# Float64 weights to float32: a byte-to-integer operation on ACT in place of two operations on DVE

## The chip, the cores and the metric

One core of one Trainium2 chip runs the kernel. The metric is the device time in microseconds (us) of one execution; lower is better.

## What is computed

A local and a downsampled attention over 4 batches x 8 heads x 576 positions x 64, then a gated feed-forward layer, then a second one with a layer norm. Only the weights of the last two matter for the change. They reach the kernel as float64:

```python
k = np.maximum(xk @ w_k, 0.0)            # xk: 2304 x 512, w_k: 512 x 1024
v = k * k @ w_v                          # w_v: 1024 x 512
r = 1.0 / (1.0 + np.exp(-(xr @ w_r)))    # w_r: 512 x 512
x = r * v
...
ch = np.maximum(xn @ w_ch1, 0.0) @ w_ch2 # w_ch1: 512 x 2048, w_ch2: 2048 x 512
out = x + ch
```

## The kernel before

**Weights.** Every weight matrix is cut into tiles of 128 x 512: 4 of `w_r`, 8 of `w_k`, 8 of `w_v`, 16 each of `w_ch1` and `w_ch2`, together 52. `load_f32` brings one in as raw float64 (512 KB) into a buffer called `w64` (in the trace `w`, and the order listings number it), of which there are two. It then makes a float32 tile `wf` (two buffers) out of the high and the low 32-bit word of each number: an absolute value on ACT, then four DVE operations that clamp, shift and mask the high word, put the top three bits of the low word under it, and put the sign on top. `load_split` splits `wf` into a rounded part (name ending in `h`) and a remainder (`l`), since every matrix product is three products of float32r parts (lines L741 to L743). The first 20 tiles, `w_r`, `w_k` and `w_v`, are needed in the first 150 us; the 32 of `w_ch1` and `w_ch2` come between 275 and 446 us.

**The rest of the start.** The attention of the first batch (four units of two heads) must be through before the first product of the feed-forward layer: its results are added into `xT` (L725), mixed with the previous position into `tmu` (L765) and split into `xr`, `xk` (L769). Then come `psr` (with `w_r`), `psk` (with `w_k`) and `psv` (with `w_v`) in PSUM, between them the attention of later batches. Where PE would have nothing to do early on, small products called `warm` (L417) are put in.

**Order.** A planner (`Plan`) holds all operations with an engine, a cost and a due time, and lists them; operations that two engines can do (copies, remainders) go where the plan has them end sooner. Each engine runs its own list strictly in order. All DMAs are issued from one queue, SP, also in order: a load of a weight waits there until DVE is done with the buffer, and everything listed behind it waits too.

Of the kernel before, what the change touches and what calls it, by code (L numbers as in the profile page):

```python
# [3 lines left out]

# [6 lines left out]
F32 = mybir.dt.float32  # L11
F32R = mybir.dt.float32r
U32 = mybir.dt.uint32
BF16 = mybir.dt.bfloat16
AF = mybir.ActivationFunctionType
ALU = mybir.AluOpType
# [2 lines left out]

P = 128  # L20
NEG = -8.0e9

TINY = struct.unpack("<f", struct.pack("<I", 896 << 20))[0]


PRM = dict(
# [34 lines left out]
class Plan:  # L61
# [15 lines left out]
    def add(self, eng, cost, prio, fn, r=(), w=(), lat=0.0, port=False, thin=False):  # L77
        ways = [(eng, cost, fn, port)] if isinstance(eng, str) else eng
        op = Op(len(self.ops), ways, prio, lat, thin)
        for kind, items in (("r", r), ("w", w)):  # L80
            for it in items:
                b, key = it if isinstance(it, tuple) else (it, None)
                keys = set(b.writer) | set(b.readers) if key is None else {key, None}
                for kk in keys:
                    if kk in b.writer:
                        op.deps.add(b.writer[kk])
                    if kind == "w":
                        op.deps.update(b.readers.get(kk, ()))
                if b not in op.bufs:
                    op.bufs.append(b)  # L90
        for it in r:
            b, key = it if isinstance(it, tuple) else (it, None)
            b.readers.setdefault(key, []).append(op.i)
        for it in w:
            b, key = it if isinstance(it, tuple) else (it, None)
            if key is None:
                b.writer.clear()
                b.readers.clear()
            b.writer[key] = op.i
            b.readers[key] = []  # L100
        op.deps.discard(op.i)
        self.ops.append(op)
# [138 lines left out]
def c_act(n, psum=False, ap=0):  # L241
    return (0.05 if psum else 0.093) + n / 1200 + 0.093 * ap


def c_dve(n, fast=False):
    return 0.066 + n / (1920 if fast else 960)
# [6 lines left out]
def c_dma(nbytes, small=False):  # L253
    return max(0.41, nbytes / 360e3 * (2 if small else 1))
# [3 lines left out]
def attn_moe_kernel(  # L258
# [15 lines left out]
    nc = tc.nc  # L274
# [18 lines left out]
    add = plan.add  # L293
# [22 lines left out]
    nc.vector.tensor_reduce(isum[:, :24], ident[:, :96].rearrange("p (s r) -> p s r", r=4), axis=AX.X, op=ALU.add)  # L316
    identb = const.tile([P, P], BF16, name="identb")
    nc.vector.tensor_copy(identb, ident)
    maskb = const.tile([P, G, 32], BF16, name="maskb")
    nc.gpsimd.memset(maskb, 0.0)  # L320
# [50 lines left out]
    def load_f32(src, f, prio):  # L371
        if src.dtype == F32:
            add("SP", c_dma(P * 2048), prio - PRM["wld"], lambda: nc.sync.dma_start(out=f(), in_=src), w=[f], lat=2.2)
        else:
            w64 = Buf(wk, [P, 512, 2], U32, "w64", 2)
            add("SP", c_dma(P * 4096), prio - PRM["wld"],
                lambda: nc.sync.dma_start(out=w64().rearrange("p a b -> p (a b)"), in_=src.bitcast(U32)),
                w=[w64], lat=2.2)
            add("ACT", c_act(512), prio, lambda: nc.scalar.activation(f(), w64().bitcast(F32)[:, :, 1], AF.Abs),  # L379
                r=[w64], w=[f])  # L380
            fu = lambda: f().bitcast(U32)
            add("DVE", c_dve(512, True), prio, lambda: nc.vector.tensor_scalar_max(f(), f(), TINY), w=[f],  # L382
                port=True)
            add("DVE", c_dve(512, True), prio,
                lambda: nc.vector.tensor_scalar(fu(), fu(), 3, 0x3FFFFFF8, op0=ALU.logical_shift_left,
                                                op1=ALU.bitwise_and), w=[f], port=True)
            add("DVE", c_dve(512), prio,
                lambda: nc.vector.scalar_tensor_tensor(fu(), w64()[:, :, 0], 29, fu(),  # L388
                                                       op0=ALU.logical_shift_right, op1=ALU.bitwise_or),
                r=[w64], w=[f], port=True)  # L390
            add("DVE", c_dve(512), prio,
                lambda: nc.vector.scalar_tensor_tensor(fu(), w64()[:, :, 1], 0xC0000000, fu(),  # L392
                                                       op0=ALU.bitwise_and, op1=ALU.bitwise_or),
                r=[w64], w=[f], port=True)

    def load_split(src, slot, name, prio, pool=None):
        if pool is None:
            hi = Buf(wp, [P, 512], F32R, f"s{slot}h", 1, f"{name}h")
            lo = Buf(wp, [P, 512], F32R, f"s{slot}l", 1, f"{name}l")
        else:  # L400
            hi = Buf(pool, [P, 512], F32R, f"{name}h", 1)
            lo = Buf(pool, [P, 512], F32R, f"{name}l", 1)
        f = Buf(wk, [P, 512], F32, "wf", 2)
        load_f32(src, f, prio)
        add(copy(512, hi, f), 0, prio, None, r=[f], w=[hi])
        add(either(512, lambda e: e.tensor_tensor(lo(), f(), hi().bitcast(F32), op=ALU.subtract)), 0, prio, None,
            r=[f, hi], w=[lo])
        return hi, lo
# [801 lines left out]
    def prep_prio(T, step):  # L1210
# [7 lines left out]
        w=[glb], lat=2.2)  # L1218
# [141 lines left out]
```

## Time and profile before

| | |
|---|---|
| device time, median of 3 runs | 786.23 us (785.75 to 789.48) |
| time of the profiled execution | 791.19 us |
| its span, first to last instruction | 789.4 us |
| busy: PE / DVE / ACT / POOL | 762.4 / 531.6 / 374.3 / 116.1 us |
| moved by DMA | 120.31 MB |

The profiled execution is 1.8 us longer than its own span and 5.0 us over the median. PE's busy time counts matmuls that overlap and the `warm` products, so it is not PE at its peak.

### The profile page before, as it was taken

What the parts mean: (1) busy time and instruction counts of PE and PEld (TensorE: products, weight loads), DVE (VectorE), ACT (ScalarE), POOL (GpSimd) and SP (SyncE); (2) the same over time, 40 slices, a digit from 0 to 9 for tenths busy, and PEclk for the clock granted to TensorE, in tenths of its full rate; (3) what the DMA queues carried; (4) which work ended last, traced back from release to release, by engine and by line L of the source; (5) the groups of instructions that cost most, each with busy time, mean ns of one, the idle gap of its engine ahead of it and who ended that gap; (6) DMA issues with size and microseconds to landing.
All of it is one profiled execution on the core that took longest, in us unless ns stands there. A gap on an engine that the chain in (4) does not pass through costs nothing.

```text
span 789.4 us, 15623 instructions
## 1 busy us (share of the span) xinstructions
PE 762.4 (97%) x5940; PEld 667.3 (85%) x5940; DVE 531.6 (67%) x1094; ACT 374.3 (47%) x854; POOL 116.1 (15%) x162
## 2 busy tenths in 40 slices
PE   7798789999999999999999999999999999999998
PEld 7677667788788798888999999998988888898986
DVE  5799698974775768998889986737553355333233
ACT  4678676765865766858644334411421131111110
POOL 6332243312320100100001022200100030000000
PEclk9789898999999999999999999999999999999999
DMA  8899799453540033446475698887854346544422
GB/s 214 176 165 166 151 174 150 102 97 81 124 52 22 34 119 128 159 149 167 129 190 169 196 328 224 252 321 263 196 152 112 117 121 216 171 120 113 128 68 80
DMA packets 187199, 120.31 MB, mean 152 GB/s; under 512 B 129524, under 2 KB 154996, under 8 KB 187124
## 3 DMA queue, kind: packets, MB, share of 16 engines
q1 hardware_dynamic: 187124, 119.32, 58.8%
q8 instruction: 47, 0.77, 0.4%
q14 instruction: 28, 0.23, 0.1%
HBM read 90.44 MB, written 28.84 MB: 151 GB/s over the span
## 4 chain that ended last, share of the span: by engine, by line
PE 82%; DVE 7%; DMA 5%; ACT 3%; issue 2%; SPq 1%; DVEq 0%; ACTq 0%
PE pso L742 8%; PE pso L743 8%; PE pso L741 8%; PE psh L741 7%; PE psh L743 7%; PE psh L742 7%; PE psk L741 4%; PE psk L743 4%; PE psk L742 4%; PE psv L741 4%; PE psv L742 4%; PE psv L743 4%; PE pv L711 2%; DMA w<-in_moe_w_k_dram 2%; PE ds L619 2%
## 5 line engine op out<-in xcount | busy, mean ns | idle before, releaser
L741 PE MATMUL psh<-xn,sa 128*128 128x384 f32 x224 | 75.7, 338 | 1.8 <-ACT u L359 1.0
L743 PE MATMUL psh<-xn,sa 128*128 128x384 f32 x224 | 75.5, 337 | 0.0
L742 PE MATMUL psh<-xn,sa 128*128 128x384 f32 x224 | 75.3, 336 | 0.0
L741 PEld LDWEIGHTS psh<-xn,sa 128*128 128x128 f32 x224 | 42.1, 188 | 7.0 <-ACT u L359 1.4
L379 ACT ACTIVATE wf<-w 128x512 f32<-128x512 f32 x52 | 34.7, 668 | 27.1 <-DMA w<-in_moe_w_ch_dram 10.2
L742 PEld LDWEIGHTS psh<-xn,sa 128*128 128x128 f32 x224 | 42.1, 188 | 3.9
L743 PEld LDWEIGHTS psh<-xn,sa 128*128 128x128 f32 x224 | 42.1, 188 | 0.0
L367 ACT ACTIVATE c22h<-t 128x384 fp32r<-128x384 f32 x16 | 8.4, 525 | 66.2 <-DVE t L1136 66.2
L367 ACT ACTIVATE kr<-psk 128x384 f32<-128x384 f32 x46 | 22.5, 490 | 34.7 <-PE psk L743 29.0
L388 DVE SCALAR_TENSOR_TENSOR wf<-w,wf 128x512 uint32<-128x512 uint32 x52 | 37.0, 714 | 0.5
L392 DVE SCALAR_TENSOR_TENSOR wf<-w,wf 128x512 uint32<-128x512 uint32 x52 | 36.7, 707 | 0.4
L806 DVE TENSOR_TENSOR kl<-kr,kh 128x384 fp32r<-128x384 f32 x38 | 21.7, 570 | 20.3 <-ACT kr L805 20.1
L382 DVE TENSOR_SCALAR wf<-wf 128x512 f32<-128x512 f32 x52 | 24.1, 464 | 15.8 <-ACT wf L379 15.6
L367 ACT ACTIVATE hh<-psh 128x384 fp32r<-128x384 f32 x32 | 15.7, 489 | 35.9 <-PE psh L743 35.3
L417 PE MATMUL warm<-identb 128*128 128x128 bf16 x308 | 27.6, 244 | 3.9 <-issue 2.1
L572 POOL TENSOR_TENSOR v<-v 72x512 f32<-72x512 f32 x16 | 21.7, 1357 | 57.6 <-DMA v<-in_v_dram 50.0
L417 PEld LDWEIGHTS <-identb 128*128 128x128 bf16 x308 | 22.2, 111 | 5.3 <-issue 2.7
L363 ACT COPY PT<-pT 32x288 f32<-32x288 f32 x54 | 23.1, 428 | 6.8 <-PE pv L711 5.8
L367 ACT ACTIVATE c11h<-psh 128x384 fp32r<-128x384 f32 x16 | 7.9, 491 | 38.6 <-PE psh L743 38.5
L803 ACT ACTIVATE kh<-kr 128x384 fp32r<-128x384 f32 x48 | 25.1, 524 | 0.8
L1113 DVE SCALAR_TENSOR_TENSOR c11l<-psh,c11h 128x384 fp32r<-128x384 f32 x16 | 8.8, 553 | 24.4 <-ACT c11h L367 24.2
L854 POOL TENSOR_TENSOR raw<-raw 128x384 f32<-128x384 f32 x5 | 5.9, 1181 | 128.3 <-DVE xn L1081 67.7
(772 smaller groups left out, 2396.8 us busy)
## 6 DMA issues: line engine op xcount, KB each, us to landing
sa<-s_dram SPq DMA_DIRECT2D x112, 256.0 KB
w<-in_moe_w_ch_dram SPq DMA_DIRECT2D x32, 512.0 KB
s_dram<-s SPq DMA_DIRECT2D x16, 512.0 KB
vw<-in_v_dram SPq DMA_DIRECT2D x62, 96.0 KB
v<-in_v_dram SPq DMA_DIRECT2D x16, 288.0 KB
x_dram<-r SPq DMA_DIRECT2D x18, 256.0 KB
x1t<-x_dram SPq DMA_DIRECT2D x6, 768.0 KB
z_dram<-x1t SPq DMA_DIRECT2D x18, 256.0 KB
```

Of the source, the lines that this page charges most:

```text
L363: return [("ACT", c_act(n), lambda: nc.scalar.copy(dst(), src()), False), ("DVE", c_dve(n, True), lambda: nc.vector.tensor_copy(dst(), src ...
L367: return [("ACT", c_act(n, True), lambda: nc.scalar.activation(dst(), src(), AF.Relu), False), ("DVE", c_dve(n), lambda: nc.vector.tensor_ ...
L379: add("ACT", c_act(512), prio, lambda: nc.scalar.activation(f(), w64().bitcast(F32)[:, :, 1], AF.Abs), r=[w64], w=[f])
L382: add("DVE", c_dve(512, True), prio, lambda: nc.vector.tensor_scalar_max(f(), f(), TINY), w=[f], port=True)
L388: lambda: nc.vector.scalar_tensor_tensor(fu(), w64()[:, :, 0], 29, fu(), op0=ALU.logical_shift_right, op1=ALU.bitwise_or),
L392: lambda: nc.vector.scalar_tensor_tensor(fu(), w64()[:, :, 1], 0xC0000000, fu(), op0=ALU.bitwise_and, op1=ALU.bitwise_or),
L417: nc.tensor.matmul(warm()[:, :P], identb, identb, start=True, stop=True)
L572: lambda: nc.gpsimd.tensor_tensor(v4()[:, :, 0:2, :], v4()[:, :, 0:2, :], v4()[:, :, 2:4, :], op=ALU.add),
L741: nc.tensor.matmul(ps, lh, rh, start=start, stop=False, skip_group_check=more)
L742: nc.tensor.matmul(ps, lh, rl, start=False, stop=False, skip_group_check=more)
L743: nc.tensor.matmul(ps, ll, rh, start=False, stop=stop, skip_group_check=more)
L803: add("ACT", c_act(C), prio, lambda: nc.scalar.activation(kh(), kr(), AF.Square), r=[kr], w=[kh])
```

## The change

Of the four DVE operations of a tile, the two `TENSOR_SCALAR` (the clamp at L382; shift and mask at L385) are gone. The absolute value on ACT now also multiplies by 2^-112, which sets the exponent's offset right. A new ACT operation reads the top byte of the low word (every eighth byte), scales it by 7.45/255 and writes it, as a whole number, over the low word in the `w64` buffer. The first remaining DVE operation shifts the scaled magnitude left and takes that number in with an OR; the second takes the sign bit, as before. DMAs, buffers, planner parameters and all other operations stay.

```diff
-            add("ACT", c_act(512), prio, lambda: nc.scalar.activation(f(), w64().bitcast(F32)[:, :, 1], AF.Abs),
-                r=[w64], w=[f])
+            add("ACT", c_act(512), prio, lambda: nc.scalar.activation(
+                f(), w64().bitcast(F32)[:, :, 1], AF.Abs, scale=2.0 ** -112), r=[w64], w=[f])
+            add("ACT", c_act(512), prio, lambda: nc.scalar.activation(
+                w64()[:, :, 0], w64().bitcast(U8).rearrange("p a (b c) -> p a b c", c=4)[:, :, 0, 3], AF.Copy,
+                scale=7.45 / 255), w=[w64])
             fu = lambda: f().bitcast(U32)
-            add("DVE", c_dve(512, True), prio, lambda: nc.vector.tensor_scalar_max(f(), f(), TINY), w=[f],
-                port=True)
-            add("DVE", c_dve(512, True), prio,
-                lambda: nc.vector.tensor_scalar(fu(), fu(), 3, 0x3FFFFFF8, op0=ALU.logical_shift_left,
-                                                op1=ALU.bitwise_and), w=[f], port=True)
             add("DVE", c_dve(512), prio,
-                lambda: nc.vector.scalar_tensor_tensor(fu(), w64()[:, :, 0], 29, fu(),
-                                                       op0=ALU.logical_shift_right, op1=ALU.bitwise_or),
+                lambda: nc.vector.scalar_tensor_tensor(fu(), fu(), 3, w64()[:, :, 0],
+                                                       op0=ALU.logical_shift_left, op1=ALU.bitwise_or),
                 r=[w64], w=[f], port=True)
             add("DVE", c_dve(512), prio,
-                lambda: nc.vector.scalar_tensor_tensor(fu(), w64()[:, :, 1], 0xC0000000, fu(),
+                lambda: nc.vector.scalar_tensor_tensor(fu(), w64()[:, :, 1], 0x80000000, fu(),
                                                        op0=ALU.bitwise_and, op1=ALU.bitwise_or),
```

The planner knows the new costs, so it also lists things differently. On DVE, before the change, this stands around the first two additions into `xT` (L725); `w_673`, `w_707` and `w_979` are the buffers of the sixth, seventh and eighth tile, and nothing of the eighth stands in these rows:

```order
L725 TENSOR_TENSOR xT_185<-pv,ups 128x288
L388 SCALAR_TENSOR_TENSOR wf<-w_673,wf 128x512
L385 TENSOR_SCALAR wf<-wf 128x512
L392 SCALAR_TENSOR_TENSOR wf<-w_673,wf 128x512
L388 SCALAR_TENSOR_TENSOR wf<-w_707,wf 128x512
L725 TENSOR_TENSOR xT_185<-pv,ups 128x288
L406 TENSOR_TENSOR wk20l<-wf,wk20h 128x512
L392 SCALAR_TENSOR_TENSOR wf<-w_707,wf 128x512
L765 SCALAR_TENSOR_TENSOR tmu<-xT_185,omr,tmu 128x384
```

And this stands there after the change, where `w_657` and `w_776` are the buffers of the seventh and the eighth tile:

```order
L388 SCALAR_TENSOR_TENSOR wf<-wf,w_657 128x512
L392 SCALAR_TENSOR_TENSOR wf<-w_657,wf 128x512
L631 TENSOR_REDUCE mxd<-ds 128x3
L388 SCALAR_TENSOR_TENSOR wf<-wf,w_776 128x512
L406 TENSOR_TENSOR wk10l<-wf,wk10h 128x512
L392 SCALAR_TENSOR_TENSOR wf<-w_776,wf 128x512
L633 TENSOR_SCALAR mxd<-mxd 128x3
L604 TENSOR_REDUCE mx<-sc 128x6 x2
L607 TENSOR_TENSOR e<-sc,mx 128x192 x2
L725 TENSOR_TENSOR xT_185<-pv,ups 128x288 x2
```

All eight tiles of `w_r` and of the first half of `w_k` now stand ahead of the first addition into `xT`, where the sixth and seventh were half done and the eighth came after it.

On ACT, before the change, this stands around the twelfth tile (`w_1504`), with the copies of the attention (`PT`, `pdT`) right behind its absolute value:

```order
L367 ACTIVATE kr<-psk 128x384
L379 ACTIVATE wf<-w_1504 128x512
L363 COPY PT<-pT 32x12x24 x4
L363 CAST wk21h<-wf 128x512
L803 ACTIVATE kh<-kr 128x384
L674 ACTIVATE pdT<-tp 72x288
```

After the change the twelfth tile is `w_1497`, and its byte operation (L383) stands three rows behind the absolute value (L381):

```order
L803 ACTIVATE kh<-kr 128x384
L381 ACTIVATE wf<-w_1497 128x512
L361 COPY PT<-pT 32x12x24 x2
L805 ACTIVATE kr<-kr 128x384
L383 ACTIVATE w_1497<-w_1497 128x512
L674 ACTIVATE pdT<-tp 72x288
```

The copies stay near the tile, and one more operation per tile stands among them.

## Rows read from the trace of the kernel before

**Rows 1.** Stretches of the span: busy us of each engine (instructions), clock, DMA share, GB/s.
```profile
0.00:40.00 40.00, 31.29 (x617) 27.58 (x618) 27.34 (x59) 22.11 (x55) 19.82 (x44) 0.89 0.85 195
40.00:64.00 24.00, 20.70 (x350) 17.00 (x349) 21.59 (x47) 17.93 (x49) 7.18 (x8) 0.90 0.95 161
64.00:100.00 36.00, 31.79 (x413) 26.55 (x412) 28.84 (x63) 27.79 (x74) 10.12 (x17) 0.91 0.88 155
100.00:120.00 20.00, 16.93 (x303) 13.05 (x304) 19.60 (x42) 14.94 (x40) 7.43 (x10) 0.99 1.01 182
120.00:138.00 18.00, 18.00 (x126) 14.74 (x123) 15.00 (x31) 11.87 (x31) 6.85 (x8) 0.82 0.93 151
138.00:150.00 12.00, 10.56 (x246) 8.16 (x245) 11.70 (x26) 7.75 (x17) 3.15 (x6) 1.00 0.69 123
150.00:789.00 639.00, 633.11 (x3912) 560.25 (x3911) 407.54 (x832) 271.87 (x591) 61.54 (x71) 1.00 0.52 149
```

**Rows 2.** Chain that ended last, 69 to 152 us: start us, us, what.
```profile
69.46 6.63 DMA w<-in_moe_w_k_dram
76.11 0.67 ACT wf L379
...
78.26 7.58 DMA w<-in_moe_w_k_dram
85.93 0.66 ACT wf L379
...
108.05 0.67 ACT wf L379
...
149.07 0.61 DVE wv7l L406
...
149.73 0.50 PE psv L742
```

**Rows 3.** Groups of instructions, DVE, ACT and POOL: xcount | busy us, mean ns | idle before.
```profile
L388 DVE SCALAR_TENSOR_TENSOR wf<-w,wf 128x512 uint32<-128x512 uint32 x52 | 37.0, 714 | 0.5
...
L382 DVE TENSOR_SCALAR wf<-wf 128x512 f32<-128x512 f32 x52 | 24.1, 464 | 15.8 <-ACT wf L379 15.6
L385 DVE TENSOR_SCALAR wf<-wf 128x512 uint32<-128x512 uint32 x52 | 23.4, 452 | 0.3
...
L379 ACT ACTIVATE wf<-w 128x512 f32<-128x512 f32 x52 | 34.7, 668 | 27.1 <-DMA w<-in_moe_w_ch_dram 10.2 <-DMA w<-in_moe_w_k_dram 8.2 <-DMA w<-in_moe_w_r_dram 6.5
...
L572 POOL TENSOR_TENSOR v<-v 72x512 f32<-72x512 f32 x16 | 21.7, 1357 | 57.6 <-DMA v<-in_v_dram 50.0 <-DMA vw<-in_v_dram 4.1 <-DVE wf L385 3.5
```

**Rows 4.** Timeline of DVE, 44 to 144 us: start us, us, instruction.
```profile
44.49 0.46 DVE L725 TENSOR_TENSOR xT<-pv,ups 128x288 f32<-128x288 f32 x1 [0.83 <-PE pv L711]
...
45.47 0.42 DVE L385 TENSOR_SCALAR wf<-wf 128x512 uint32<-128x512 uint32 x1
45.80 0.68 DVE L392 SCALAR_TENSOR_TENSOR wf<-w,wf 128x512 uint32<-128x512 uint32 x1
...
58.17 0.68 DVE L392 SCALAR_TENSOR_TENSOR wf<-w,wf 128x512 uint32<-128x512 uint32 x1
...
117.07 1.21 DVE L382 TENSOR_SCALAR wf<-wf 128x512 f32<-128x512 f32 x1
...
143.66 0.42 DVE L385 TENSOR_SCALAR wf<-wf 128x512 uint32<-128x512 uint32 x1
143.99 0.41 DVE L765 SCALAR_TENSOR_TENSOR tmu<-xT,omk,tmu 128x192 f32<-128x192 f32 x1
```

**Rows 5.** Timeline of ACT at the twelfth tile: start us, us, instruction [idle before].
```profile
85.93 0.66 ACT L379 ACTIVATE wf<-w 128x512 f32<-128x512 f32 x1 [2.92 <-DMA w<-in_moe_w_k_dram]
86.49 1.74 ACT L363 COPY PT<-pT 32x288 f32<-32x288 f32 x4
```

**Rows 6.** Waits of the DMA queue SP, 40 to 150 us: us, times, longest us.
```profile
SPq L377 <- DVE wf L392: 9.1, 7, 3.0
```

**Rows 7.** The same, 0 to 150 us.
```profile
SPq L377 <- DVE wf L392: 19.9, 11, 4.4
```

More of the change, by code (lines that the diff above doesn't have):

```diff
@@ L1 @@
 import heapq
-import struct
 from contextlib import ExitStack
@@ L13 @@
 U32 = mybir.dt.uint32
+U8 = mybir.dt.uint8
 BF16 = mybir.dt.bfloat16
@@ L21 @@
 NEG = -8.0e9
-TINY = struct.unpack("<f", struct.pack("<I", 896 << 20))[0]
 PRM = dict(
```

## The prediction

> **What bounds the kernel now.** I read the stretches of the span first [rows 1]. From 150 us on PE is busy for 633.11 of 639 us at full granted clock, while DVE has 407.54 and ACT 271.87 us of work there: whatever the change does on those two engines after 150 us lies beside PE. This holds for 32 of the 52 tiles, those of `w_ch1` and `w_ch2`. The first 150 us are another kernel. PE is there with gaps and filler products and at a clock of 0.82 to 0.91 in most stretches, and two other things are nearly full: DVE, with 21.59 of 24 us between 40 and 64, 19.60 of 20 between 100 and 120 and 11.70 of 12 between 138 and 150, and the 16 DMA engines, with shares of 0.85, 0.95, 0.88, 1.01 and 0.93 until 138 us. So the time is decided by when the first 20 weight tiles and the attention of the first batches are through; from there on PE's work is fixed, and a start that is shorter by a microsecond shortens the end by the same.
>
> The chain that ended last says how these meet [rows 2]. It goes through the load of two tiles of `w_k` (6.63 and 7.58 us), each followed by the tile's absolute value on ACT; it passes ACT once more that way at 108.05 us, and it leaves DVE for good at 149.07 us with the remainder of the last tile of `w_v`, on which PE's `psv` waits until 149.73. The waits of the DMA queue close the circle: SP stood 11 times, 19.9 us in all, with a weight load in front because DVE's last operation on the buffer, L392, was not through [rows 7]; seven of these, 9.1 us, fall after 40 us [rows 6]. With two buffers, slow conversion of a tile delays the load of the next but one.
>
> **The change, part by part.** Removed: 2 x 52 DVE operations of 464 and 452 ns [rows 3], together 47.5 us of DVE. Added: 52 ACT operations. Kept: the two `SCALAR_TENSOR_TENSOR`. The first has its operands exchanged, but shape, stride and kind are those of the 714 ns row [rows 3]; I cost that at nothing, and if the exchange did cost, it would stand in DVE's path at every tile. The scale inside the absolute value is an immediate of the same instruction; I cost it at nothing too, since ACT would be its cover nowhere: a longer L379 would show in the three places where the chain passes ACT.
>
> Only the first 20 tiles count. (1) *DVE's own path.* From 44.49 us to the eighth tile's L392 at 58.17, from 100 to 120, and from 138 to 150, DVE has next to no gaps [rows 1, 4], so an operation taken out moves all behind it. In these runs lie eleven of the removed ones. Neighbours overlap, so what goes is the time from one start to the next: L385 at 45.47 is followed at 45.80, the one at 143.66 at 143.99, that is 0.33 us [rows 4]. Ten of them cost that; one, at 117.07, takes 1.21 us, less the same overlap of 0.09 is 1.12. Sum 10 x 0.33 + 1.12 = 4.4 us won.
>
> (2) *ACT's path.* The trace has no operation that reads bytes and writes whole numbers. From below: the same engine, 128 x 512, read at the same stride of eight bytes, is L379; at 85.93 it holds ACT for 0.56 us until the next start [rows 5], and nothing suggests less for more. From above the slowest row of such a size, on POOL, with 1.357 us [rows 3]. I take 0.56, the row of the same engine and stride, and keep 1.36 for the range. The chain passes L379 three times before 150 us [rows 2], and the new operation holds what stands next on ACT, the copies that the attention's products wait for: 3 x 0.56 = 1.7 us lost (4.1 at the upper price).
>
> (3) *Buffers.* A tile comes out of conversion sooner by 0.464 + 0.452 less 0.56, that is 0.36 us, if its other waiting stays. At SP's seven waits after 40 us this is 7 x 0.36 = 2.5 us won; before 40 us I count nothing, because there DMA is at 0.85 and DVE at 27.34 of 40 us, and the attention's loads stand between. Bounds: nothing, if the DMA engines have no room; with the upper ACT price 7 x (0.916 - 1.36) = -3.1; and 10 us, if half of the 19.9 us goes with half of the DVE operations.
>
> Sum: 4.4 - 1.7 + 2.5 = 5.2 us. On the profiled execution this is 791.19 to 786.0; that execution is 5.0 us over the median of the runs, so I apply the difference to the median: 786.23 - 5.2 = 781.0. Low end: 4.4 - 1.7 + 10 = 12.7 won, 773.5. High end of the costs alone: 4.4 - 4.1 - 3.1 = -2.8, 789.0.
>
> **Rivals.** *The DMA engines keep what DVE gives.* For it: shares of 0.88 to 1.01 between 40 and 138 us [rows 1], and two loads of 512 KB on the chain itself. A tile that is converted sooner then only queues sooner. Against it: 0.69 after 138, 0.88 between 64 and 100, and SP's waits, in which no weight load was under way for that buffer. What is left is the last stretch and part of one before, two or three of the eleven places, against ACT's three: about 1 us won, 785.
>
> *ACT is too dear.* At 1.36 us a byte operation the sum is the high end, 789.0. ACT has 102.4 us of work in the first 150 us (the sum of its column in [rows 1]); 20 x 1.36 would make it 129.6, above DVE's then, 124.1 - 20 x 0.916 = 105.8. Against it: every ACT row of this size is near 0.6. The Trainium skill ("ScalarE: Activation LUTs", Rules for kernel authors) says that multiplications belong on VectorE, not ScalarE. By that rule the move itself would be the mistake and this rival the result; the trace doesn't agree so far, with two DVE operations of 464 and 452 ns against one of 668 ns.
>
> *The new order waits for weights* (the other side). All eight early tiles stand on DVE ahead of the first addition into `xT`, which now runs at 44.49 us; the eighth tile's L392 starts at 58.17 and ends at 58.85 [rows 4]. If the loads come no sooner, the first `xT` starts 14.4 us later. Taken off that: the eighth tile's operations no longer follow (0.714 + 0.68 + 0.464 + 0.452 = 2.3 us), 3.4 us of term (1) after 100 us, 2.5 of term (3); 1.7 of term (2) comes on top. 14.4 - 2.3 - 3.4 - 2.5 + 1.7 = 7.9 us lost, 794.1. It decides (over 0.5%, which is about what a measurement of this kernel can tell from no change, 3.9 us) from a delay of 10.4 us. For it: the listing, and DMA at 0.85 before 40 us. Against it: SP's waits in that time, 19.9 - 9.1 = 10.8 us, are all for buffers that the shorter conversion frees sooner.
>
> *More than the sum.* If the waiting between a tile's steps goes with the steps, the low end holds: 773.5. For it: two of four in-order stops on a full engine vanish, and the L382 at 117.07 took 1.21 us where the mean is 464 ns [rows 3, 4]. GpSimd's work beside it goes easier too: L572 stood 3.5 us behind L385 [rows 3]. The Trainium skill ("GPSIMD Engine Reference", Key points) says that GpSimd shares its SBUF interfaces with VectorE and contends with VectorE instructions in a two-port mode or with two SBUF inputs. By that rule part of it stays, since the two operations that remain read two inputs from SBUF; a long L382 agrees with contention, and says nothing of how much of it goes.
>
> **How the numbers follow.** The sum of the three terms, 781.0: 0.43, with a range of its own from 778 to 784. DMA keeps it: 0.20. ACT too dear: 0.11. The new order waits: 0.13. More than the sum: 0.13. The range takes in the low end and the high end of the costs with half a microsecond of the spread of the runs: 774 to 789.5; it leaves out the new order that waits and the last bit of the gain, under 2 in 10. Faster by over 0.5% (under 782.3) are the last case and most of the first: 0.50. Within 0.5%: the rest of the first, the DMA case and most of the dear ACT: 0.35. Slower: 0.15.
>
> **What the profile after would show.** Right: 104 DVE operations fewer, an ACT row of 52 with about 0.6 to 0.7 us; the last remainder of `w_v` near 144 us instead of 149.07; SP's waits for L392 under 19.9 us; after 150 us the same PE-bound stretch. Wrong: that row above 1 us; DMA shares of 1 with the last tile still at 149 us; the first `xT` after 50 us with DVE idle behind a weight; or a PE stretch after 150 us that changes by more than the start does, since I hold the new order there to be neutral.

## The result and the profile after

The changed kernel takes 793.76 us in the median of nine runs (791.67 to 797.51), the kernel before 785.48 us beside it: a ratio of 1.0113 [1.0079, 1.0147]. The change makes the kernel slower by 8.3 us (8.9 by the ratio); 781.0 was predicted, and the time lies above the range.

The page of the profile after, its span and busy times, and its four groups of the weights' conversion (columns as in [rows 3]):

```profile
span 793.7 us, 15637 instructions
## 1 busy us (share of the span) xinstructions
PE 761.8 (96%) x5959; PEld 664.6 (84%) x5959; DVE 503.3 (63%) x1001; ACT 393.6 (50%) x889; POOL 123.9 (16%) x169
...
L388 DVE SCALAR_TENSOR_TENSOR wf<-wf,w 128x512 uint32<-128x512 uint32 x52 | 37.7, 724 | 16.7 <-ACT w L383 14.0
...
L381 ACT ACTIVATE wf<-w 128x512 f32<-128x512 f32 x52 | 35.0, 672 | 20.2 <-DMA w<-in_moe_w_ch_dram 11.6
...
L392 DVE SCALAR_TENSOR_TENSOR wf<-w,wf 128x512 uint32<-128x512 uint32 x52 | 37.4, 720 | 0.6
...
L383 ACT ACTIVATE w<-w 128x512 uint32<-128x512 uint8 x52 | 34.6, 665 | 0.0
```

The operations cost what the prediction gave them: bytes to integers 665 ns, the absolute value with its scale 672, the exchanged operands 724. So the loss is not in the duration of any of them.

Two profiles of before are at hand, the one of [rows 1 to 7] and a second one (run e0 below, same program). They differ by 4.8 us, and 4.5 of it comes within the first 150 us. I use the second as the base, because its span (784.6 us) fits the median. By stretch: its length, busy us of PE, PEld (loading of weights into PE), DVE, ACT and POOL with their instructions, granted clock, DMA share and GB/s, first before (second profile), then after:

```profile
0.00:150.00 150.00, 129.92 (x2049) 107.28 (x2050) 128.71 (x275) 104.92 (x272) 57.75 (x92) 0.94 0.89 171
150.00:280.00 130.00, 130.00 (x1430) 110.82 (x1429) 86.05 (x198) 89.37 (x228) 25.82 (x42) 1.00 0.35 72
...
350.00:460.00 110.00, 109.87 (x548) 98.71 (x547) 100.16 (x204) 57.04 (x111) 6.93 (x6) 1.00 0.64 183
```

```profile
0.00:150.00 150.00, 131.98 (x2080) 108.03 (x2080) 125.37 (x261) 113.37 (x288) 55.01 (x96) 0.95 0.87 171
150.00:280.00 130.00, 126.67 (x1402) 107.31 (x1401) 79.82 (x186) 84.80 (x212) 22.85 (x36) 0.99 0.34 71
...
350.00:460.00 110.00, 105.62 (x517) 94.39 (x516) 92.16 (x170) 63.07 (x123) 17.09 (x14) 0.98 0.65 190
```

On PE, before has no idle microsecond between 150 and 280 us, after 3.3; between 350 and 460 before lacks 0.13, after 4.4. The loss lies where I expected none. What PE waited for between 150 and 470 us, first before (second profile), then after (us in total, times, longest):

```profile
PE psk L741 <- ACT r L785: 0.7, 1, 0.7
```

```profile
PE psr L741 <- ACT r L785: 4.4, 2, 3.7
PE tp L670 <- ACT PT L361: 2.5, 1, 2.5
PE sc L593 <- issue: 0.7, 1, 0.7
PE psk L741 <- DVE kr L366: 0.7, 1, 0.7
PE psr L743 <- DVE xrl L769: 0.3, 1, 0.3
```

The first layer works through its 2304 positions in six chunks of three tiles. Both long waits stand where one chunk goes over to the next. **The first border**, on PE, of after (start us, us, instruction, [idle before]):

```profile
151.48 0.95 PE L619 MATMUL ds<-kd,qd 64*64 64x144 f32 x12
154.96 0.82 PE L670 MATMUL tp<-isum,pd 128*72 128x128 f32 x6 [2.53 <-ACT PT L361]
155.70 0.59 PE L741 MATMUL psr<-wr0h,xrh 128*128 128x512 f32 x1
156.09 0.63 PE L742 MATMUL psr<-wr0l,xrh 128*128 128x512 f32 x1
```

and on DVE and ACT at the same time:

```profile
150.52 1.87 DVE L824 TENSOR_TENSOR r<-psv,r 128x512 f32<-128x512 f32 x3
...
153.41 0.56 DVE L651 STREAM_TRANSPOSE pT<-e 128x384 f32<-128x384 f32 x1
```

```profile
154.00 0.87 ACT L361 COPY PT<-pT 32x288 f32<-32x288 f32 x2 [0.40 <-DVE pT L651]
155.05 0.60 ACT L785 ACTIVATE r<-psr 128x512 f32<-128x512 f32 x1 [0.17 <-DMA x_dram<-r]
```

In the new order PE has the products `psr` of two tiles ahead of the last `psv`. So `psv` ends late, and its three multiplications L824 stand together on DVE at 150.52, ahead of the transposition that `tp` waits for. That they are the cause is read from the lists and not shown (see e8 below). PE's clock is then granted at its lower level (1.2 GHz): `psr` products stand about 0.43 us apart until 159.45, and 0.23 after. **The fifth border**, in the chain that ended last of after:

```profile
356.89 0.23 PE psr L743
357.12 0.23 PE psv L741
357.35 0.23 PE psv L742
357.57 0.24 PE psv L743
...
357.84 0.70 DVE r L824
...
358.56 3.60 DMA x_dram<-r
...
362.24 0.61 ACT r L785
...
362.89 0.50 PE psr L741
```

The same pattern. There are three `r` buffers; the exponential L785 of the next chunk needs one, each is free only after its store, and the store comes after the last `psv`. The third `psr` needs a PSUM bank that L785 empties. Before has the last `psv` of two tiles ahead of `psr`, and its stores begin at 354.74 (first profile).

To place the loss I count matmul work (columns over 2.4 GHz) and take the instant at which each kernel has done the same amount, minus that of before's second profile. These are differences worked out from single profiled executions, in us; the head gives the base's own instant:

```
                              141.2  164.1  300.9  345.3  373.0  454.8  724.4
before, first profile          +4.0   +4.5   +4.7   +4.6   +4.2   +4.2   +4.8
after                          -3.1   +2.7   +2.7   +3.0   +8.9   +8.9   +9.2
```

After is 3.1 us ahead at 141 us, loses 5.8 at the first border and 5.9 at the fifth.

### The profile page after: what moved, and what is told of

It reads as the page before. It is cut to its first block, busy times and chain, and to the rows that moved or that the text cites. A ratio compares the mean times of both kernels' runs of the same rounds, so it can differ in the third digit from the quotient of the medians.

```text
span 793.7 us, 15637 instructions
## 1 busy us (share of the span) xinstructions
PE 761.8 (96%) x5959; PEld 664.6 (84%) x5959; DVE 503.3 (63%) x1001; ACT 393.6 (50%) x889; POOL 123.9 (16%) x169
## 4 chain that ended last, share of the span: by engine, by line
PE 76%; DVE 8%; DMA 5%; ACT 4%; issue 3%; SPq 2%; POOL 1%; DVEq 0%; ACTq 0%; POOLq 0%
PE pso L742 8%; PE pso L743 8%; PE pso L741 8%; PE psh L741 7%; PE psh L743 7%; PE psh L742 7%; PE psk L741 4%; PE psk L743 4%; PE psk L742 4%; PE psv L741 3%; PE psv L742 3%; PE psv L743 3%; PE psr L741 2%; PE psr L743 2%; PE psr L742 2%
## 5 line engine op out<-in xcount | busy, mean ns | idle before, releaser
L388 DVE SCALAR_TENSOR_TENSOR wf<-wf,w 128x512 uint32<-128x512 uint32 x52 | 37.7, 724 | 16.7 <-ACT w L383 14.0
L806 DVE TENSOR_TENSOR kl<-kr,kh 128x384 fp32r<-128x384 f32 x42 | 24.2, 577 | 35.8 <-ACT kr L805 35.5
L381 ACT ACTIVATE wf<-w 128x512 f32<-128x512 f32 x52 | 35.0, 672 | 20.2 <-DMA w<-in_moe_w_ch_dram 11.6
L392 DVE SCALAR_TENSOR_TENSOR wf<-w,wf 128x512 uint32<-128x512 uint32 x52 | 37.4, 720 | 0.6
L383 ACT ACTIVATE w<-w 128x512 uint32<-128x512 uint8 x52 | 34.6, 665 | 0.0
L959 DVE SCALAR_TENSOR_TENSOR hl<-psh,hh 128x384 fp32r<-128x384 f32 x32 | 17.5, 547 | 19.8 <-ACT hh L365 19.8
L805 ACT ACTIVATE kr<-kr 128x384 f32<-128x384 f32 x47 | 24.6, 522 | 0.8
```

What stands on the lines that cost most here:

```text
L383: add("ACT", c_act(512), prio, lambda: nc.scalar.activation(w64()[:, :, 0], w64().bitcast(U8).rearrange("p a (b c) -> p a b c", c=4)[:, :, ...
L388: lambda: nc.vector.scalar_tensor_tensor(fu(), fu(), 3, w64()[:, :, 0], op0=ALU.logical_shift_left, op1=ALU.bitwise_or),
L805: ("ACT", c_act(C), lambda: nc.scalar.activation(kr(), kr(), AF.Square), False)], 0, prio, None, w=[kr])
L806: add(either(C, lambda e: e.tensor_tensor(kl(), kr(), kh().bitcast(F32), op=ALU.subtract)), 0, prio, None, r=[kr, kh], w=[kl])
```

## Experiments

A number after "before" is the median of the runs of before measured beside that kernel. A gain or loss in us is the ratio less 1, times that median, and brackets behind it are its interval in us. What is said of a border is in the terms of the table above: how far a kernel is behind before's second profile, at 141 and 164 us for the first border, at 345 and 373 us for the fifth. In the expectations of the first four runs, A reads: the exchange wins at the start, and the border in the new order loses more; B: the operations themselves lose, in any order; C: the new order loses, but not at that border alone. From the fifth run on each expectation says what its letter means there.

**The operations without their order, and the order without the operations.** e1 keeps before's list; the new instructions are issued in the old ones' places:

```
-  add("ACT", ..., lambda: activation(f(), w64()..., AF.Abs), ...)
+  add("ACT", ..., abs_and_byte, ...)       # both, back to back
-  tensor_scalar_max ... / tensor_scalar ...
+  add("DVE", ..., lambda: None, ...)       # twice: nothing issued
```

> The new operations in the old order: the planner sees the five operations of before, the absolute value's place issues absolute value and byte operation back to back, the places of the two removed DVE operations issue nothing. Theory A (the loss is made by the planner's new order at the border between the fifth and the sixth chunk of the first layer, where psr waits for an r buffer; the exchange of operations itself wins about 3 us at the start): no wait of psr for ACT's r over 1 us after 340 us, and 780 to 784 us against 785.5 of before. Theory B (the byte operation on ACT costs more than the two DVE operations gave): 787 us or more. Theory C (the new order at the start costs the time): also 780 to 784, but then undoing the border alone would win nothing.

787.53 us, before 784.59: ratio 1.0045 [1.0023, 1.0066]. The exchange wins nothing even in before's own order; it loses 3.5 us [1.8, 5.2], which is within B's range and not in A's or C's. e2 is the reverse: after's plan, nothing issued at the byte operation's place, clamp, shift and combination in a row on DVE:

> The old operations in the new order: the planner sees the four operations of after, the byte operation's place issues nothing, clamp, shift and mask are issued on DVE right ahead of the first bitwise operation. Theory A: the wait of psr near 360 us is there as in after, and the start wins nothing, so 792 to 798 us. Theory B: the ACT operation is gone, so like before, 784 to 788. Theory C: as A, 792 to 798.

812.95 us, ratio 1.0375 [1.0343, 1.0407]. That is far over every theory. I take it that a list drawn up for two operations is bad for four; it says nothing on the price of the new ones. But the two runs together tell where the borders' loss comes from. In e1 no border loses (from +0.3 to -0.4 at the first, from +0.2 to +1.1 at the fifth), in e2 both do (from +1.7 to +8.0, from +11.3 to +18.0), much as in after (5.8 and 5.9). So both losses came with the list, and not with the operations in before's list; e2 loses time elsewhere too, which makes its half of this the weaker one. Where e1 loses its 3.5 us its trace does not show.

**The border by hand.** e3 moves, in after, the fifth chunk's last `psv`, multiplications and stores ahead of the sixth chunk's first `psr`; e4 moves them behind the first eight `psr` groups in before:

```
+  return seq[:n] + up + [i for i in seq[n:] if i not in up]                           # e3
+  return [i for i in seq[:exp] if i not in down] + down + seq[exp:]                   # e4
```

> The changed kernel with one thing moved: the last products psv of the fifth chunk, the three multiplications of r and their stores stand ahead of the sixth chunk's first psr instead of behind its first eight products; all else is listed as in after. Theory A: the wait of 3.7 us and the 1.2 GHz stretch behind it go, 5 to 6 us less than after, 787.5 to 789. Theories B and C: as after, 792 to 795.

798.12 us, ratio 1.0171 [1.0137, 1.0205], above the ranges of all three theories. The wait for the store went, but the exponentials now stand behind a layer norm's statistics on ACT, and past the border PE is as late as in after (+0.5 at 345 us, +8.8 at 373):

```profile
363.59 0.20 ACT L921 ACTIVATE rstd<-var 128x3 f32<-128x3 f32 x1 [5.75 <-DVE var L920]
...
365.22 0.57 ACT L795 ACTIVATE r<-psr 128x512 f32<-128x512 f32 x1
```

> The kernel before with one thing moved the other way: the last products psv of the first two tiles of the fifth chunk, their multiplications and stores stand behind the first eight products psr of the sixth chunk, as in after. Theory A: a wait of psr for ACT's r of 3 to 4 us and a stretch at 1.2 GHz appear near 360 us, 4 to 6 us over before, 789.5 to 791.5. Theories B and C: as before, 784 to 787.

787.64 us, ratio 1.0052 [1.0025, 1.0079], and in the trace +2.2 at 345 us, +7.5 at 373. The median lies between A's range and that of B and C. So the arrangement at that border, put into before by itself, does cost: 4.1 us [2.0, 6.2] by the ratio, 5.3 in the trace, whose execution was the longest of the eleven (794.32 us). That supports the reading of the chain. As a remedy it fails, and further cleaning by hand made it worse. e7 adds to e3 that the statistics sink behind the last `r`; e8 puts the last `psv` first at all five borders; e9 adds to e8 that the three `r` operations follow their tile's last product at once:

> The changed kernel with both in-order blockers at the border of the fifth to the sixth chunk taken away: the psv products, multiplications and stores of the fifth chunk ahead of the sixth chunk's first psr product, and the second layer norm's statistics behind the sixth chunk's last operation on r. Theory B, that the loss is these waits in ACT's list: 6 to 9 us less than the version that moved only the stores (798.1), so 785 to 791 us, and the progress of PE stays ahead of before across the border. Rival C, that the time is lost all over the new order and the border only shows it: above 794.

> The changed kernel with the psv products, multiplications and stores of each chunk ahead of the next chunk's first psr product, at all five borders between chunks. Theory B, in its second form: the new order loses at two borders, 5.5 us at the first (the tp wait and the low clock behind it) and some 6 at the fifth, and the one cause is psr put ahead of the last psv. The first border's loss goes and the fifth stays as in the version that moved the fifth border alone (798.1): 791 to 795 us. Rival C, that what stands in the way is always something else in line: 796 and above.

> The version with psv ahead everywhere, and on ACT the three operations on r put right behind the last psr product of their tile in the order, so that no statistics, casts or weights stand ahead of them. Theory B: the wait at the fifth border goes too, 4 to 6 us more, and the start's 3 us are kept: 783 to 789 us. Rival C: other operations on ACT are now late and PE waits for them, 794 and above.

799.05 (1.0158 [1.0124, 1.0191]; before 786.89), 804.25 (1.0229 [1.0188, 1.0269]) and 815.08 us (1.0364 [1.0323, 1.0405]; before 786.75). Each edit uncovers what stood behind: in e7 PE waits 4.3 us for `r` behind weights' absolute values on ACT; in e8 6.6 us; in e9 4.8 and 4.2 us for the attention's copies and 4.0 for `r`. The expectations of 785 to 791, 791 to 795 and 783 to 789 fell. At the first border e8 loses as much as after (from -1.5 to +4.4), now in waits of the attention's products `ds` and `tp`; so it isn't shown that `psr` ahead of the last `psv` makes the loss there. A wait that the chain shows can be the cause of a loss, and its removal still win nothing.

**The exchange in halves, before's order kept.** e5 issues the absolute value of each tile twice, e6 leaves out the two DVE operations and adds nothing on ACT (the low three bits of each weight are left out):

```
+  nc.scalar.activation(f(), w64()..., AF.Abs)                                         # e5: once more
-  tensor_scalar_max ... / tensor_scalar ...                                           # e6
+  scalar_tensor_tensor(fu(), fu(), 3, zero..., logical_shift_left, bitwise_or)        # e6
```

> The kernel before, in its own order, with the absolute value of each of the 52 tiles issued twice in a row on ACT (the output is unchanged). Theory A, the prediction's: one more operation of ACT costs 0.56 us on each of the few tiles that ACT holds up, so 785 to 787.5 us against 784.6. Theory D, that the 3 us by which the new operations in the old order were slower are the price of ACT's extra operation: 787 to 791.

> The kernel before, in its own order, with the two DVE operations of each tile (clamp, shift and mask) left out and no byte operation in their place: the first combining operation shifts and takes zero for the low part, so the low three bits of each weight are left out. Theory A: the two terms DVE's own path and Buffers, 4.4 and 2.5 us, are won without any loss on ACT: 777 to 781 us. Theory D: DVE's operations were hidden by the loads and by ACT, 783 to 786.

> The kernel before, unchanged, under another name, to see how far two profiles and two sets of runs of one program differ. All theories: a ratio of 1.000 within 0.003. If the profile's start (the first 150 us) differs by 2 us or more from the first profile's, the gain that the first comparison showed there is the profile's scatter, not the change.

e5: 795.86 us against 786.89, ratio 1.0118 [1.0084, 1.0152], 9.3 us lost, more than either theory had. e6: 786.68 us, 0.9985 [0.9959, 1.0010], 1.2 us won and 3.2 at the very best, nearer to D than to A. e0: 785.31 us, 0.9991 [0.9963, 1.0018], and its profile's start is 4.5 us faster than that of [rows 1 to 7]. So a lead at the start that one profile shows can be scatter, as e0's expectation says; that a new list can be ahead at 141 us rests on five of them, some further below (after -3.1, e3 -5.7, e12 -3.5, e16 -4.2, e17 -5.9), all ahead of the faster profile; e15 is not (+6.2).

By itself the removed DVE work was worth next to nothing, and the added ACT work cost 9.3 us. But the two don't add: that would be 8.1 us lost, and e1, which has both in the same list, loses 3.5. With the operation added on ACT, the two DVE operations are worth some 6 us. Which tiles carry ACT's price is told by doubling on the 32 late ones (e10) or the 20 early ones (e11) alone:

```
+  if name[:2] in ("w1", "w2"): nc.scalar.activation(f(), w64()..., AF.Abs)            # e10; e11: not in
```

> The kernel before, in its own order, with the absolute value issued twice for the 32 tiles of the channel-mix weights alone, which are converted after 275 us. Theory D in its second form: the whole price of ACT's extra operation, 9 us over 52 tiles, falls where the prediction held it to lie beside PE: 792 to 797 us. Rival, the prediction's, that it is free after 150 us: 785 to 788.

> The same with the 20 tiles of the start alone. Theory D in its second form: 785 to 788 us, since the loads set the start's pace. Rival, the prediction's own two cases: its term of 1.7 us, or 9.3 us by the rival in which ACT is too dear at the start, 787 to 796.

e10: 794.44 us, 1.0108 [1.0065, 1.0152], 8.5 us. e11: 789.16 us, 1.0024 [1.0001, 1.0047], 1.9 us [0.1, 3.7]. e10 is in D's range, e11 in the rival's. In the early tiles the operation costs about what term (2) says; in the late ones, held to be free, 8.5 us. How, the end of the conversion in e10 shows; first what PE waits for between 150 and 470 us, then the chain:

```profile
PE pso L747 <- DVE hl L963: 2.9, 1, 2.9
PE psk L745 <- ACT r L789: 1.4, 1, 1.4
PE psv L747 <- DVE kl L810: 1.1, 1, 1.1
...
```

```profile
449.07 0.63 ACT w215h L363
...
449.72 0.69 DVE w215l L410
450.41 3.61 DVE a L858 x6
454.02 0.60 DVE s L854
454.62 0.60 DVE a L858
455.23 0.60 DVE s L854
455.83 1.81 DVE a L858 x3
457.63 0.48 DVE hl L963
...
458.16 0.64 PE pso L747
```

In before (second profile) the same remainder of the last tile starts at 442.99:

```profile
442.99 0.69 DVE L406 TENSOR_TENSOR w215l<-wf,w215h 128x512 fp32r<-128x512 f32 x1 [0.22 <-ACT w215h L363]
...
450.82 1.02 DVE L959 SCALAR_TENSOR_TENSOR hl<-psh,hh 128x384 fp32r<-128x384 f32 x2
```

A tile's steps follow each other through load, ACT, DVE, ACT, DVE with two buffers, so one step more makes each tile late, and in the end 6.7 us late. Behind the last tile stand twelve combinations of weights on DVE, and behind these `hl`, for which PE waits. Between 150 and 460 us it does not help that ACT is idle for a third to half of the time: the work of PE hangs on instructions that stand behind the weights' in the lists.

This is what an added operation costs, and not how after loses. Where two DVE operations go as the one on ACT comes, the last remainder is not late, neither in e1 (first line) nor in after:

```profile
443.50 0.69 DVE L409 TENSOR_TENSOR w215l<-wf,w215h 128x512 fp32r<-128x512 f32 x1
```

```profile
442.50 0.68 DVE L406 TENSOR_TENSOR w215l<-wf,w215h 128x512 fp32r<-128x512 f32 x1
```

**Where the new list is drawn.** e12 makes the exchange for the 20 early tiles alone, e13 for the 32 late ones, each planned anew:

```
+  if name[:2] not in ("w1", "w2"): (new operations)                                   # e13: in
+  else: (old operations)
```

> The new operations for the 20 tiles of the start alone, planned anew; the 32 tiles of the channel-mix weights keep the old ones. Theory F, that the loss is ACT's extra operation on the late tiles: 780 to 786 us, the start's few us won. Theory G, that the loss is the luck of any new list (psr ahead of the last psv at the borders): 790 and above, with a loss at one border or another.

> The new operations for the 32 late tiles alone, planned anew. The start's list may change little, since the late tiles come after it. Theory F: 789 to 795 us, most of the change's loss. Theory G: anywhere from 785 to 800, by what the new list has at the borders.

e12: 791.03 us against 785.16, 1.0083 [1.0052, 1.0114]. e13: 792.11 us, 1.0092 [1.0064, 1.0121]. In the table's terms e12 goes from -3.5 to +2.8 at the first border and has nothing at the fifth (+3.6, +3.2); e13 is +2.6 and +2.1 at the first and goes from +2.4 to +8.5 at the fifth. Each half brings one border's loss. e12 is in theory G's range; e13 is in both. The times don't add up (6.5 and 7.2 us against 8.9 for after), so this rests on single profiles.

Last, orders alone. e14 is before, e15 and e17 are after, with one number changed in the planner: the time that it assumes for the absolute value. e16 is after with 21 of the planner's numbers (the expectation says 20) moved in small steps, kept whenever the planner's own count of the end came earlier:

```
-  add("ACT", c_act(512), prio, ... AF.Abs ...)
+  add("ACT", c_act(512) + 0.1, prio, ... AF.Abs ...)      # e14, e17; e15: - 0.1
```

> The kernel before with all its operations, and one number of its planner changed: the absolute value of a weight tile is planned 0.1 us longer. Nothing that is computed changes, only the order. Theory G: the order of before is better than orders near it, so 790 to 810 us. Theory F: within 4 us of before, 783 to 791.

> The changed kernel with its absolute value planned 0.1 us shorter, nothing else. Theory G: another draw from the same scatter, 788 to 812 us, and as likely above the changed kernel's 794 as below it. Theory F: within 4 us of 794.

> The changed kernel with its own operations and another order: 20 of the planner's numbers are changed in small steps, kept wherever the end that the planner itself counts came earlier. Its own count of the end goes from 738.8 to 731.8 us; it is 731.3 for before. Theory G, that the loss is the order and not the operations: 783 to 790 us. Theory F, that the operations cost it wherever they stand: 791 and above, since the count leaves out what the chip adds.

> The changed kernel with its absolute value planned 0.1 us longer, nothing else; the planner's own count of the end is 737.3 us. Theory G: another draw of an order, 788 to 803 us. Theory F: within 4 us of the changed kernel's 794.

e14: 802.83 us, 1.0231 [1.0199, 1.0264]. e15: 800.89, 1.0199 [1.0168, 1.0230]. Both are in theory G's range alone. e17: 792.56 against 784.95, 1.0100 [1.0045, 1.0156], in both ranges. e16: 790.41, 1.0059 [1.0030, 1.0088]; it lands between the two theories' ranges. With every operation of before in place, another list alone costs 18 us. PE's longest waits of e14 from 130 to 345 us:

```profile
PE sc L587 <- DVE e L607: 4.2, 1, 4.2
PE psk L741 <- ACT r L785: 1.9, 1, 1.9
PE sc L587 <- ACT pd L636: 1.6, 1, 1.6
...
```

The loss at the fifth border is more than the luck of a list, though. Each list drawn for the new costs of the late tiles has it (after 5.9 us, e13 6.1, e15 6.1, e16 3.7, e17 5.9, and e2 with the old operations 6.7); of those drawn for the old costs of the late tiles none has (before, e12 -0.4, e14 -0.2).

No kernel with the new operations came to before's time; the nearest is e1, with before's own list, 0.45% above it.

## Why the prediction was wrong

**The step that failed** is the first sentence on the bound: that whatever the change does on DVE and ACT after 150 us lies beside PE, and with it the last, that the new order there is neutral. What I had read was right: PE is full from 150 us on [rows 1], in the second profile without one idle microsecond up to 280 us. What I made of it was not. A stretch that is full because a list hides every step behind PE can't be shortened by less work elsewhere, but it can be lengthened by a later step or by a worse list. e10 measured the first, 8.5 us for one more operation of ACT at each of 32 tiles. e14 shows the second: with no operation changed it goes from 6.4 us behind at 141 us to 15.3 at 724, 9 of its 18 us. In after it is the list: 5.8 us at the first border and 5.9 at the fifth, which e2 has too, with that list and the old operations, and e1 has not, with the new operations in the old list. The operations in the old list cost 3.5 us, the list by subtraction another 5.3 (1.0113 against 1.0045). That split is no more than a subtraction, since the same list with the old operations costs 29 us.

**Term (1), DVE's own path, 4.4 us won, and term (3), buffers, 2.5 us:** mis-sized together, as terms of their own (beside the added ACT operation, e5 less e1, the two DVE operations were worth some 6 us). Without the two operations and with nothing in their place e6 won 1.2 us of 6.9, and the interval ends at 3.2. Term (3) was also too large on its own rows: it takes the operations' full durations, where term (1) takes 0.33 us from one start to the next; with 0.33 a tile is out sooner by 0.10 us, and the term is 0.7. Buffers did come free sooner in e6: SP's waits for the conversion fell to

```profile
SPq L381 <- DVE wf L395: 14.3, 7, 5.9
```

against 19.9 in [rows 7] and 20.2 in the second profile. This gave next to nothing, so the waits of an issuing queue were no measure of time on the path. In after itself they stayed at 19.7. The full DVE stretches of [rows 1, 4] were also partly that execution's: its start was 4.5 us slower than the second profile's.

**Term (2), ACT's path, 1.7 us lost:** about right for the early tiles (e11: 1.9), and the price of 0.56 to 0.67 us was right. The count of three was one short: the chain passes L379 at 4.60 us too. Above all the term left out 32 tiles of 52. The rule of the Trainium skill ("ScalarE: Activation LUTs", Rules for kernel authors) that multiplications belong on VectorE goes by the price per element; the sign came out as by that rule, but no such price shows here. The byte operation took 665 ns, against 916 for the two DVE operations and 1.36 us in the rival, and the loss was not at the start.

**The rivals.** *The new order waits for weights* has the right sign and the nearest time (794.1), but by luck, since the place is wrong: the first `xT` started at 44.40 us, and the eighth tile was through at 41.05 instead of 58.85. *DMA keeps it* is near what e6 shows for the DVE half, and says nothing of the rest. *More than the sum* fell.

**What was to show it right or wrong.** The ACT row of 52 came as foretold. The last remainder of `w_v` started at 132.6 us, against 144.5 in before's second profile, 12 us sooner and far more than the 5 foretold; and PE was ahead for it by only 3 us at 141. What told the result is the last sign of the list: a PE stretch after 150 us that changes by more than the start.

**What stays open.** Whether some list makes the new operations as fast as before. e16 recovers about half, by a search on the planner's own count of the end. That count is 731.3 for before, 731.8 for e16, 737.3 for e17, 738.8 for after and 741.9 for e14, which is the order of the measured times; but e15 has 738.5 and is 7 us slower than after, and at an almost equal count e16 is still 0.6% above before. Why the start's gain of 3 us goes at the first border, whether by that list or because DVE is full there in any case (10.00 of 10 us from 150 to 160 in before's second profile), was not told apart. The five lists named above that are ahead at 141 us are all behind or level at 164 (after +2.7, e3 +0.3, e12 +2.8, e16 +0.2, e17 +0.1), so none of them kept the gain.

## What to carry to other kernels

Where one engine is full and all others are scheduled around it, ask of each added step who stands behind it in the in-order lists, not how idle its engine is. Where a planner draws the lists from assumed costs, a change of operations is also a new list: measure the new operations once in the old list and the old operations once in the new and in a slightly changed list, before anything is said of the operations themselves. And take a second profile of the kernel before: here its start alone differed by 4.5 us, which is nearly the whole gain that I summed from it.

## What the runs showed of the hardware

Bytes read at a stride of eight bytes and written as 32-bit integers cost ACT 665 ns at 128 x 512, no more than the absolute value in float32 (672 ns). After PE's two long waits in after its clock was granted at the lower of the two levels (1.2 GHz) for some time, so that `psr` products stood up to 0.43 us apart instead of 0.23. At the first border, after an idle time of 2.53 us, this held from 155.70 to 159.45 us (mean granted clock 0.54 of full speed there, 0.83 over 150 to 160): nine products in 3.75 us where 2.07 would do, 1.7 us on top of the wait.
